# A two-stage kernel on one core: twelve intermediate tiles kept on the chip, and a new written order for its first sixty microseconds

## The chip, the cores and the metric

The kernel runs on one core of one Trainium2 chip. The metric is the device time of one execution in microseconds (us); smaller is better. The core has five engines, each with its own queue in program order: TensorE (PE; its weight loads are shown apart as PEld), VectorE (DVE), ScalarE (ACT), GpSimd (POOL) and SyncE (SP, which here issues every DMA). PE writes only to PSUM, which has eight banks of 128 x 512 floats; ACT and DVE take the results out of it.

## The reference

A retention layer (a linear attention with a decay per head) is followed by a two-layer network with SiLU. All is float32.

```python
# q, k, v: batch 4, heads 8, 768 positions, head size 64
gamma = 1.0 - 2.0 ** (-5.0 - np.arange(H))
for t in range(S):
    state = gamma * state + outer(k[:, :, t], v[:, :, t])
    y[:, :, t] = scale * q[:, :, t] @ state
x = y.transpose(0, 2, 1, 3).reshape(3072, 512)
h = x @ w_in                      # 512 x 2048
out = (h / (1 + np.exp(-h))) @ w_out   # 2048 x 512
```

## The kernel before

Retention is computed by *units*: unit n is chunk n // 4 (of six chunks of 128 positions) of batch n % 4, so there are 24. For each unit the letters of the written order stand for:

- `T(n)`: PE transposes k and q into PSUM (`kp`, `qp`), and ACT copies them out (`kt`, `qt`). `K(n)` on DVE, or `KA(n)` on ACT in eight pieces, scales k; `Q(n)` on DVE scales qt.
- `SC(n)`: PE makes sums of k and v and the scores. `A(n)`, three calls: DVE masks the scores (`am`), and the sums go into `mid` and then `state`. `SC` of the next unit uses the same banks (tag `s`), so it waits for these.
- `YA(n)`, `YB(n)`: PE's products that make y; between them stands a fence, a POOL instruction that waits for the last matmul of YA and lets YB begin.
- `X(n)`, four calls: ACT copies y out, ACT makes the first of three parts of `xt`, and DVE the second and third. (Each float32 product is done as three passes of a rounded format, so each operand is split into three parts.)
- `W(i)`: one step of turning slice i of w_in (given as 64-bit floats) into its three parts, on ACT and DVE, eleven calls in all.

The first layer has 96 *groups* (c, f): chunk c of all four batches (512 rows) times slice f of 16 of the hidden width. A group is twelve matmuls of 128 x 512 into two banks, `ha` and `hb`. `P(n)` issues such a product in the early order and `CL(n)`, three calls, closes it: ACT copies ha out with a factor (L744), DVE subtracts hb (L749), ACT applies SiLU (L754). The result, g, is 256 KB, and `put_g` stores it to DRAM (L760). Products and the transposed k share three banks in turn (`turn`). Once all groups are done, the second layer reads each g back (L773), splits it (L805 to L808) and multiplies it by w_out (L1088), chunk by chunk, 128 x 512 outputs in two banks, `oa` and `ob`. The last two slices of the last chunk are issued batch by batch at the end (L1102), so that the outputs of the first three batches are taken out meanwhile.

The order of the work: PE's order is written out by hand throughout. In the first part, up to `early_order.close()` (units 0 to 9, groups (0,0), (0,1), (0,2) and (1,0)), so is that of SP, DVE, ACT and POOL: each engine runs its instructions in the order of the source. After that a planner orders those four, held by `queue(...)` and `issue_after(...)`, which put instructions behind a named one. The later units come in *visits* between groups: a visit m does the transposes of unit m and YA of unit m - 2 in its first half, and SC of unit m - 1 and YB of m - 2 in its second. `steps` lists the remaining groups: (1,1), (1,2), (0,3), (1,3), (0,4), (1,4), then from step 6 on (0,5), (1,5), (2,0), (0,6) and so on.

On-chip room: k, q and v of units 0 to 7 share the slots of w4 to w11, the third parts of which these units fill before those slices of w_in are converted (`load`, `early`); those of later units have two or three buffers each. g has three buffers (tag `hs`).

Some narrow and full matmuls on zeros (`narrow`, `fill`) only keep PE busy at the start and in gaps.

Of the kernel before, what the change touches and what calls it, by code (L numbers as in the profile page):

```python
# [34 lines left out]
def kernel(  # L35
# [28 lines left out]
    nc = tc.nc  # L64
# [81 lines left out]
    early = {}  # L146
# [27 lines left out]
    def load_w(i):  # L174
# [8 lines left out]
        if i < NF:  # L183
            to = t.rearrange("p (i o f) -> o p i f", o=2, f=n)
            src = w_in[:, ts(i, n)].rearrange("(i o p) f -> o p i f", o=2, p=128)
            nc.sync.dma_start(out=to[0], in_=src[0])
# [139 lines left out]
    for n in range(EARLY - 2):  # L326
        for name in "kqv":
            load(name, n)
        if n in (0, 3):
            load_w(n // 3)  # L330
# [128 lines left out]
    FILL_P = {(0, 0): 1, (1, 0): 2}  # L459

# [277 lines left out]

    def close_in(*of):
        list(close_steps(*of))  # L740

    def close_steps(c, f, ha, hb):
        hs = hpool.tile([128, NT], FP32, tag="hs", name=f"g_{c}_{f}")
# [11 lines left out]
        pending.append((c, f, hs))  # L755

    def put_g(keep):
        while len(pending) > keep:
            c, f, g = pending.pop(0)
            stored[:] = [nc.sync.dma_start(out=g_dram[c, f], in_=g).ins]  # L760
# [58 lines left out]

    def T(n):  # L820
        stage_t(n)
# [36 lines left out]
    idle[:] = [banks("y", "idle")[:, 0]]  # L858
    narrow(idle[0], 39)
    fill(idle[0], 2)  # L860
    narrow(idle[0], 39)
    T(0), K(0)
    nc.scalar.activation(out=token, in_=lgc[:1, :1], func=AF.Silu)
    SC(0), A(0), Q(0), A(0), A(0)
    W(0), W(0), W(0), W(0), W(0)
    YA(0), YB(0), X(0)
    T(1), K(1)
    W(0)
    load_w(2)
    W(0)  # L870
    X(0), X(0)
    SC(1), A(1)
    W(0)
    A(1)
    Q(1), A(1)
    T(2), K(2)
    W(0), X(0)
    W(0), W(0)
    YA(1), SC(2)
    A(2)  # L880
    YB(1), X(1)
    A(2), Q(2), A(2)
    X(1)
    T(3), K(3)
    X(1), X(1)
    YA(2), YB(2), X(2)
    SC(3), A(3), A(3), Q(3), A(3)
    X(2), W(1), W(1)
    X(2), X(2)
    YA(3), YB(3), X(3), X(3)  # L890
    W(1), W(1)
    T(4)
    X(3), X(3)
    K(4)
    W(1), W(1)
    loads(EARLY - 2), loads(EARLY - 1)
# [15 lines left out]
    P(0)  # L912
    next_chunk()
    SC(4)
    CL(0), CL(0), CL(0)
    put_g(0)
    W(1)
    T(5)
    A(4), A(4), Q(4), K(5), A(4)
    W(1), W(1)  # L920
    YA(4), SC(5), YB(4)
    loads(EARLY)
    load_w(3)
    W(2), W(1)
    A(5)
    W(1), W(2), W(2)
    X(4)
    T(6)
    P(1)
    A(5), Q(5), A(5)  # L930
    KA(6)
    W(2), W(2), W(2)
    load("k", EARLY + 1), load("q", EARLY + 1)
    load_w(4)
    W(2)
    CL(1), CL(1)
    W(2)
    YA(5), SC(6), YB(5)
    X(5)
    W(2), W(2)  # L940
    A(6)
    W(2)
    CL(1)
    put_g(0)
    T(7)
    P(2)
    load("v", EARLY + 1)
    K(7), A(6), Q(6), A(6)
    X(4), X(5), X(4), X(4)
    CL(2)  # L950
    YA(6), SC(7), YB(6)
    X(6)
    T(8)
    load("k", EARLY + 2), load("q", EARLY + 2)
    A(7), A(7), Q(7)
    next_chunk()
    K(8), A(7)
    CL(2), CL(2)
    put_g(0)
    X(5), X(5)  # L960
    X(6)
    YA(7), SC(8), YB(7)
    X(7), X(7)
    A(8)
    X(6), X(6)
    T(9)
    load("v", EARLY + 2), load("k", EARLY + 3), load("q", EARLY + 3)
    X(7), X(7)
    A(8), Q(8), A(8)
    P(NF)  # L970
    KA(9)
    CL(NF), CL(NF)
    taken[0] = 3
    begin_w()
    CL(NF)
# [4 lines left out]
    next(half_visits)  # L980
# [17 lines left out]
    behind = {x: lambda: next(half_visits) for x in pairs[:-1]}  # L998
# [24 lines left out]
    for n, (c, f) in enumerate(steps):  # L1023
# [4 lines left out]
        if n in parts:  # L1028
            behind_next.append(lambda m=parts[n]: part_t(m, taken_out[0]))
        patient[0] = steps.index((3, 0)) <= n < max(turns_at) + 2  # L1030
        product_in(c, f)
        put_g(1)
        store_w()
        if (c, f) in takes:
            take_w(taken_out[0], n < len(pairs + three) or c == NC - 1)
# [119 lines left out]
```

## Time and profile before

| | |
|---|---|
| time, three runs | 613.16 us median (612.46 to 614.77) |
| the profiled execution | span 612.6 us; no other time of it is on record |
| PE, busy | 600.9 us (98%) |
| DVE, busy | 397.1 us (65%) |
| ACT, busy | 324.5 us (53%) |
| DMA | 108.90 MB, queue 62.3% of 16 engines' span |
| stores of g, reads of g | 96 and 96, 256 KB each, 3.7 and 2.7 us from issue to landing |

A timeline row reads: start, duration, engine, line, operation, out<-in, shape, count, and in brackets the idle time of the engine before it with what ended it. An entry such as SPq is the queue of an engine; the duration of a DMA there is that of its issue, and it lands some microseconds later. "Granted clock" is the share of its full clock that PE was given; it is 1.00 all through.

### The profile page before, as it was taken

The page shows a single profiled execution, that of the slowest core. Times are in us where ns is not written, and L with a number is a line of the kernel's source. Part 1 is how long each engine was busy: PE and PEld are TensorE (multiplying, and loading weights), DVE is VectorE, ACT ScalarE, POOL GpSimd, SP SyncE. Part 2 cuts the span into 40 slices and gives each one's busy share as a digit, 9 for nine tenths or more (in the row PEclk, how much of TensorE's full clock was granted, in tenths as well). Part 3 has the DMA queues.
Part 4 walks back from the last instruction along what each step waited for, and adds up shares of the span by engine and source line. Part 5 has one row for each costly group of instructions (what it writes and reads, how often), then busy time and mean ns, then how long its engine had stood idle before and what let it go on. Part 6 is the DMA issues. An engine that isn't in the chain of part 4 may idle for free.

```text
span 612.6 us, 13713 instructions
## 1 busy us (share of the span) xinstructions
PE 600.9 (98%) x5509; PEld 495.9 (81%) x5509; DVE 397.1 (65%) x672; ACT 324.5 (53%) x598; POOL 32.9 (5%) x89
## 2 busy tenths in 40 slices
PE   8898999999999999999999999999999999999997
PEld 6686788888888888888888888888888888888886
DVE  4797898678886676766689774635545463645631
ACT  7688678678676667676698632212221322313211
POOL 3000020100021111210000000000000000000000
PEclk9999999999999999999999999999999999999999
DMA  9999976586799699998777542623524433433301
GB/s 195 209 199 231 258 214 203 160 254 188 258 231 233 154 263 263 258 291 255 248 249 267 169 138 69 206 69 106 169 72 136 137 110 97 152 123 99 107 1 69
DMA packets 144336, 108.90 MB, mean 178 GB/s; under 512 B 101137, under 2 KB 109585, under 8 KB 144273
## 3 DMA queue, kind: packets, MB, share of 16 engines
q1 hardware_dynamic: 144272, 108.03, 62.3%
q8 instruction: 43, 0.70, 0.5%
q14 instruction: 21, 0.16, 0.1%
HBM read 66.06 MB, written 36.70 MB: 168 GB/s over the span
## 4 chain that ended last, share of the span: by engine, by line
PE 92%; DMA 3%; SPq 2%; DVE 2%; issue 1%; ACT 0%; DVEq 0%
PE ha L734 28%; PE o L1088 21%; PE oa L1088 14%; PE hb L734 14%; PE ob L1088 7%; PE y L562 3%; DMA qf<-in_q_dram 2%; PE sc L504 1%; SPq L166 1%; PE sc L514 1%; DMA kqv<-in_v_dram 1%; SPq L188 1%; PE o L1102 0%; PE oa L1102 0%; PE kp L485 0%
## 5 line engine op out<-in xcount | busy, mean ns | idle before, releaser
L734 PE MATMUL ha<-xt,wi 128*128 128x512 f32 x768 | 193.0, 393 | 0.0
L734 PEld LDWEIGHTS ha<-xt,wi 128*128 128x128 f32 x768 | 142.4, 188 | 30.5 <-DVE xt L636 0.2
L1088 PE MATMUL o<-wo,gs 128*128 128x512 f32 x564 | 143.1, 389 | 0.0
L805 ACT ACTIVATE gs<-gr 128x512 fp32r<-128x512 f32 x96 | 53.2, 621 | 139.0 <-issue 138.0
L1088 PEld LDWEIGHTS o<-wo,gs 128*128 128x128 f32 x564 | 105.9, 188 | 22.0
L807 DVE TENSOR_TENSOR gs<-gr,gs 128x512 fp32r<-128x512 f32 x96 | 62.1, 684 | 94.2 <-ACT gs L805 94.2
L1088 PE MATMUL oa<-wo,gs 128*128 128x512 f32 x376 | 115.7, 389 | 0.0
L749 DVE TENSOR_TENSOR g<-g,hb 128x512 f32<-128x512 f32 x96 | 65.7, 684 | 57.6 <-ACT g L744 42.6
L734 PE MATMUL hb<-xt,wi 128*128 128x512 f32 x384 | 102.7, 389 | 0.0
L734 PEld LDWEIGHTS hb<-xt,wi 128*128 128x128 f32 x384 | 72.1, 188 | 15.1
L1088 PEld LDWEIGHTS oa<-wo,gs 128*128 128x128 f32 x376 | 70.5, 188 | 14.6
L754 ACT ACTIVATE g<-g 128x512 f32<-128x512 f32 x96 | 60.3, 629 | 37.7 <-DVE g L749 37.6
L1088 PE MATMUL ob<-wo,gs 128*128 128x512 f32 x188 | 73.1, 389 | 0.0
L744 ACT ACTIVATE g<-ha 128x512 f32<-128x512 f32 x96 | 56.7, 591 | 28.6 <-PE ha L734 19.8
L808 DVE SCALAR_TENSOR_TENSOR gs<-gs 128x512 fp32r<-128x512 f32 x96 | 62.0, 683 | 0.1
L1088 PEld LDWEIGHTS ob<-wo,gs 128*128 128x128 f32 x188 | 35.3, 188 | 7.4
L205 ACT ACTIVATE ca<-wf 128x512 f32<-128x512 f32 x32 | 21.6, 675 | 6.6 <-DVE cs L218 4.0
L522 DVE TENSOR_TENSOR am<-sc,decay 128x512 f32<-128x512 f32 x24 | 16.5, 687 | 11.4 <-PE sc L514 11.4
L1112 ACT ACTIVATE o<-o 128x512 f32<-128x512 f32 x10 | 6.0, 598 | 33.4 <-PE o L1088 33.0
L218 DVE SCALAR_TENSOR_TENSOR cs<-ca,cs 128x512 uint32<-128x512 uint32 x32 | 22.7, 710 | 0.9
L639 DVE SCALAR_TENSOR_TENSOR xt<-xt 128x512 fp32r<-128x512 f32 x28 | 19.9, 715 | 0.7
L562 PE MATMUL y<-qt,mid 64*64 64x64 f32 x376 | 19.4, 220 | 0.4 <-issue 0.4
(122 smaller groups left out, 562.2 us busy)
## 6 DMA issues: line engine op xcount, KB each, us to landing
gd<-g SPq DMA_DIRECT2D x96, 256.0 KB, 3.7
gr<-gd SPq DMA_DIRECT2D x96, 256.0 KB, 2.7
wf<-in_moe_w_out_dram SPq DMA_DIRECT2D x16, 512.0 KB, 4.7
out_dram<-o SPq DMA_DIRECT2D x23, 256.0 KB, 2.1
wf<-in_moe_w_in_dram SPq DMA_DIRECT2D x16, 256.0 KB, 4.6
wf<-in_moe_w_in_dram SPq DMA_DIRECT2D x32, 128.0 KB, 4.1
kf<-in_k_dram SPq DMA_DIRECT2D x16, 256.0 KB, 4.1
qf<-in_q_dram SPq DMA_DIRECT2D x16, 256.0 KB, 4.1
```

What stands on the lines that cost most here:

```text
L205: top = nc.scalar.activation(out=a.bitcast(FP32), in_=hi.bitcast(FP32), func=AF.Abs, scale=2.0 ** -3).ins
L218: nc.vector.scalar_tensor_tensor(out=s, in0=a, scalar=3, in1=s, op0=ALU.logical_shift_left, op1=ALU.bitwise_xor)
L562: i = nc.tensor.matmul(to[ts(e, D), o, a, :], lhsT=lhsT, rhs=rhs, start=key not in started, stop=True, skip_group_check=True).ins
L639: nc.vector.scalar_tensor_tensor(out=x[2], in0=x[1].bitcast(FP32), scalar=-1.0 / EPS, in1=x[0].bitcast(FP32), op0=ALU.mult, op1=ALU.add)
L734: nc.tensor.matmul(hb if i == 2 else ha, lhsT=w_sb[f][:, i, ts(kk, 128)], rhs=xt[c][:, i, kk, :], start=kk == 0 and i != 1, stop=kk == KIN ...
L744: copied[:] = [nc.scalar.activation(out=hs, in_=ha, func=AF.Copy, scale=ONE_E).ins]
L749: taken_out[:] = [nc.vector.tensor_tensor(out=hs, in0=hs, in1=hb, op=ALU.subtract).ins]
L754: nc.scalar.activation(out=hs, in_=hs, func=AF.Silu)
L805: nc.scalar.activation(out=t[:, 0, :], in_=g, func=AF.Copy, scale=HALF)
L807: nc.vector.tensor_tensor(out=t[:, 1, :], in0=g, in1=high, op=ALU.subtract)
L808: nc.vector.scalar_tensor_tensor(out=t[:, 2, :], in0=t[:, 1, :].bitcast(FP32), scalar=-1.0 / EPS, in1=high, op0=ALU.mult, op1=ALU.add)
L1088: nc.tensor.matmul(o, lhsT=g, rhs=wo[f][:, i, :], start=f == 0 and i != 1, stop=f == NF - 1 and i != 0)
```

## The change

- Twelve g, of groups (0,0) to (0,5) and (1,0) to (1,5), go to slots of their own in SBUF, three each in those of w7, w9, w10 and w11, and are stored later, one or two at a time in steps 6 to 17 (`keep_g`, `put_later`). A late store is placed behind the last weight load or store (`last`).
- Product (1,1) comes directly behind (1,0); the first half of visit 10, which stood between them, comes behind (1,1).
- `T(n)` is split into `TK` and `TQ`, which can be placed apart, and the order of all five engines and of the loads is another from unit 4's transposes on. Ahead of that the order is the same.
- The fillers at the start are 36 and 33 narrow matmuls rather than 39 and 39 (nine matmuls with nine weight loads).
- The last batch's left half: its last four matmuls go to a bank of their own, `last_left`. ACT takes the left half of what oa holds until then, DVE subtracts ob's, then adds the new bank's; the right half is as before.

```diff
@@ load_w
-            nc.sync.dma_start(out=to[0], in_=src[0])
+            last[:] = [nc.sync.dma_start(out=to[0], in_=src[0]).ins]
@@ beside stage_t: stage_k(n) and stage_q(n) do its two halves
@@ ahead of close_in
+    keep_g = {7: [(0, 0), (0, 1), (0, 2)], 9: [(1, 0), (1, 1), (1, 2)],
+              10: [(0, 3), (1, 3), (0, 4)], 11: [(1, 4), (0, 5), (1, 5)]}
+    kept_g = [x for i in keep_g for x in keep_g[i]]
+    homes = {}
+
+    def new_g(c, f):
+        if (c, f) not in kept_g:
+            return hpool.tile([128, NT], FP32, tag="hs", name=f"g_{c}_{f}")
+        i, = (i for i in keep_g if (c, f) in keep_g[i])
+        if i not in homes:
+            homes[i] = wpool.tile([128, 3, NT], FP32, tag=f"w{i}", name=f"gk_{i}")
+        return homes[i][:, keep_g[i].index((c, f))]
@@ close_steps and put_g
-        hs = hpool.tile([128, NT], FP32, tag="hs", name=f"g_{c}_{f}")
+        hs = new_g(c, f)
...
-        pending.append((c, f, hs))
+        (later if (c, f) in kept_g else pending).append((c, f, hs))
...
+    def put_g(keep, of=None):
+        of = pending if of is None else of
+        while len(of) > keep:
+            c, f, g = of.pop(0)
+            with tc.issue_after(last[0]) if of is later else ExitStack():
+                last[:] = stored[:] = [nc.sync.dma_start(out=g_dram[c, f], in_=g).ins]
@@ the start
-    narrow(idle[0], 39)
+    narrow(idle[0], 36)
     fill(idle[0], 2)
-    narrow(idle[0], 39)
+    narrow(idle[0], 33)
@@ the order from unit 4's transposes to the end of the early part; before
-    T(4)
-    X(3), X(3)
-    K(4)
-    W(1), W(1)
-    loads(EARLY - 2), loads(EARLY - 1)
-    P(0)
-    next_chunk()
-    SC(4)
-    CL(0), CL(0), CL(0)
-    put_g(0)
-    W(1)
-    T(5)
...
-    T(7)
-    P(2)
-    load("v", EARLY + 1)
-    K(7), A(6), Q(6), A(6)
-    X(4), X(5), X(4), X(4)
-    CL(2)
-    YA(6), SC(7), YB(6)
-    X(6)
-    T(8)
-    load("k", EARLY + 2), load("q", EARLY + 2)
-    A(7), A(7), Q(7)
-    next_chunk()
-    K(8), A(7)
-    CL(2), CL(2)
-    put_g(0)
-    X(5), X(5)
-    X(6)
-    YA(7), SC(8), YB(7)
...
@@ after
+    W(1), TK(4), TQ(4), W(1), load("k",6), load("q",6), X(3), X(3), K(4), W(1), P(0)
+    load("v",6), SC(4), next_chunk(), TK(5), W(1), TQ(5), load("k",7), W(2), W(1), Q(4), A(4)
+    load("q",7), CL(0), A(4), W(1), load("v",8), load("q",8), K(5), A(4), CL(0), load("v",7)
+    W(1), W(1), load("k",8), YA(4), SC(5), W(1), W(2), A(5), W(2), CL(0), load_w(3), W(2)
+    put_g(0), YB(4), TK(6), TQ(6), P(1), X(4), A(5), KA(6), W(2), load("q",9), W(2), W(2)
+    load("k",9), W(2), CL(1), Q(5), A(5), YA(5), SC(6), YB(5), CL(1), X(5), W(2), W(2), Q(6)
+    CL(1), X(4), W(2), A(6), TQ(7), TK(7), P(2), load("v",9), X(5), K(7), A(6), load_w(4)
+    YA(6), X(4), A(6), SC(7), YB(6), A(7), X(6), Q(7), CL(2), X(4), put_g(0), X(6), TK(8)
+    A(7), CL(2), TQ(8), load("q",10), load("k",10), CL(2), YA(7), YB(7), A(7), next_chunk()
+    K(8), X(6), X(5), X(7), X(6), put_g(0), TQ(9), X(7), X(5), TK(9), KA(9), X(7), X(7), SC(8)
+    A(8), P(NF), CL(NF), A(8), A(8), load("v",10), CL(NF), load("k",11), Q(8)
@@ the visits
-    next(half_visits)
+    behind[pairs[0]] = lambda: [next(half_visits), next(half_visits)]
@@ the loop over steps
+    put_later = {6: 1, 7: 2, 9: 1, 10: 1, 11: 1, 13: 1, 14: 1, 15: 1, 16: 1, 17: 2}
...
+        if n in put_later:
+            put_g(len(later) - put_later[n], later)
@@ the tail, last batch
-                ends += [(oa, (0, 1), slice(i * DM // 2, (i + 1) * DM // 2))
-                         for i in range(2)]
+                last_left = banks("s", "o_left")[:, 0]
+                ends += [(last_left, (0, 1), slice(0, DM // 2)), (oa, (0, 1), slice(DM // 2, DM))]
...
+            left, right = (ts(i, DM // 2) for i in range(2))
+            nc.scalar.activation(out=o[:, left], in_=oa[:, left], func=AF.Copy, scale=ONE_E)
+            nc.scalar.copy(out=o[:, right], in_=ob[:, right])
+            nc.vector.tensor_tensor(out=o[:, left], in0=o[:, left], in1=ob[:, left],
+                                    op=ALU.subtract)
+            for x, cols, op in (last_left, left, ALU.add), (oa, right, ALU.subtract):
+                nc.vector.scalar_tensor_tensor(out=o[:, cols], in0=x[:, cols], scalar=ONE_E,
+                                               in1=o[:, cols], op0=ALU.mult, op1=op)
                 nc.sync.dma_start(out=out[rows, cols], in_=o[:, cols])
```

## The prediction

> **What bounds the kernel now.** I read the page first, then TensorE's (PE's) waits, then its timeline from 25 to 70 us beside the DMA queue's, and last the tail. The page:
>
> ```profile
> span 612.6 us, 13713 instructions
> PE 600.9 (98%) x5509; PEld 495.9 (81%) x5509; DVE 397.1 (65%) x672; ACT 324.5 (53%) x598; POOL 32.9 (5%) x89
> ...
> PE   8898999999999999999999999999999999999997
> ...
> DMA  9999976586799699998777542623524433433301
> ```
>
> PE is 98% busy, and falls below 9 tenths only in the first four slices (61 us), where DMA is full, and in the last. So a gain can come only from the 11.7 us in which PE is idle, and from time in which it is busy without running at its pace. The windows say more:
>
> ```profile
> 50.00:60.00 10.00, 8.10 (x167) 6.27 (x168) 9.11 (x17) 8.81 (x24) 0.00 (x0) 1.00 0.92 235
> 60.00:70.00 10.00, 10.00 (x174) 8.00 (x174) 6.62 (x12) 6.94 (x16) 2.33 (x4) 1.00 1.03 255
> ```
>
> The columns are PE, weight loads, DVE, ACT, POOL, granted clock, DMA share, GB/s. From 60 us on PE has no gap, and before it DMA, DVE and ACT are all near full at once. PE's longest waits there:
>
> ```profile
> 52.73 0.63 PE L476 MATMUL qp<-ident,qf 128*128 128x128 f32 x4 [0.26 <-DMA qf<-in_q_dram]
> 53.20 0.59 PE L317 MATMUL ha<-zero 128*128 128x512 bf16 x2
> 53.44 2.29 PE L734 MATMUL ha<-xt,wi 128*128 128x512 f32 x8
> ...
> 58.54 0.27 PE L485 MATMUL kp<-ident,qf 64*128 64x64 f32 x1 [1.09 <-DMA qf<-in_q_dram]
> ```
>
> These are unit 9's q, first-layer group (1,0), and unit 10's q. The idle marks are not the whole loss. One undisturbed period (product 36.79 to 42.60) gives the pace: a product 2.94 us (2.72 when the next is a product too), transposes .84, SC .94, YA .75, YB .35. What PE does from unit 4's transposes (25.98) to product (1,1) (59.79) sums to 27.5 by these; it took 33.8. So 6.3 us is the most that the new order can win there. The tail:
>
> ```profile
> 607.67 1.11 PE L1102 MATMUL oa<-wo,gs 128*128 128x256 f32 x8
> 607.87 0.59 ACT L1116 COPY o<-ob 128x512 f32<-128x512 f32 x1 [0.74 <-PE ob L1102]
> 608.88 0.76 DVE L1121 SCALAR_TENSOR_TENSOR o<-oa,o 128x256 f32<-128x256 f32 x2 [0.71 <-PE oa L1102]
> ```
>
> Eight half-width matmuls, four for the left half and then four for the right. Both DVE pieces start only after the eighth ends at 608.78, though the left half was complete after the fourth (about 608.3) and ACT's copy after 608.46. Somebody who reads one half of this bank waits for the writes to the other.
>
> **The change part by part.**
>
> *Fewer fillers.* Nine narrow matmuls with their nine weight loads: 39 take 1.23 us, so 9 x .0315 = .28 us ahead of unit 0's transposes. These run at 4.25, and their k was issued at .75 and took 3.4 us to land, so the fillers were all but hidden; behind them the first SC waits another .45 for v at 6.54. Worth 0. Without that cover it would be .28.
>
> *Twelve g kept.* g(0,0) and g(0,1) no longer stand in the DMA queue ahead of unit 10's loads. By issue plus time to landing, v of unit 7 lands at 42.7 and g(0,0) at 43.5: a store takes about .78 us of the queue (g(0,1) .54, after w4's last piece). Unit 9's transposes need both k and q of 9; ahead of the later of these stand the same loads in both kernels and one store less, so it lands at 52.6 - .8 = 51.8. Unit 10's k then comes after v of 9, w4 and q of 10, (1.0 + 1.75 + 1.2 + 1.1 us by the same differences) at 56.9, against 58.5 for its q before. The stores come back as twelve issues on the SP queue in steps 6 to 17, about 87 to 118 us, where the DMA share is .5 to .7. I cost them at nothing there: PE is at its pace, and the DMA engines have 6 us free in 20. What this hides behind is the slots' re-use, the third rival.
>
> *(1,1) behind (1,0).* Product (1,1) needs nothing of unit 10. It fills the 1.09 and .34 us that PE waited for unit 10's q and k, and saves one change between products and small matmuls, 2.94 - 2.72 = .22.
>
> *The new order, from unit 4's transposes on.* Engines take their queue in order, so I follow what each waits for. Up to 31.67 (unit 5's transposes) nothing differs. Then:
> - ACT: the copy of g(0,0), at 29.95 before, now stands behind both copies of unit 5 and a piece of w2, so at 33.87, and what it held back (silu, w1's and w2's pieces) comes behind it. The scaling of unit 6's k on ACT (1.92 us) moves from 37.67 to about 39.0. SC(6) on PE needs it, and the copy of g(0,1) is queued behind it, for which DVE then stands some 2 us: SC(6) starts at 41.1 instead of 40.48.
> - That and a .2 us wait for unit 6's state puts unit 8's transposes at 48.4 instead of 47.57.
> - YA(7) now waits for mid of 7, which DVE makes after two ops more (masks and Q .60 apart, mid .33): 50.65 at its end. YB(7) follows with no SC(8) between. It must wait for the POOL fence, some .55 (unit 0's YA to YB: 9.04 + .40 to 9.73 with fillers between; last matmul to POOL to PE). Unit 9's transposes start at 51.75, just as their operands land (51.8), and end at 52.65; SC(8) ends at 53.6.
> - (1,0) needs unit 7's xt. On ACT, between YB(7)'s end and that op's end, there are now next_chunk (1.18), the copy of y (.47), a copy of unit 9 (.47) and the op itself (.63): 54.45. So (1,0) starts at 54.5 instead of 53.44.
> - From there (1,0) 2.72, (1,1) 2.94, unit 10's transposes and YA(8) together 1.50 (67.01 to 68.51 in a later visit): SC(9) at 61.66, against 62.74 before. **Gain 1.1 us**, all of which reaches the end, since PE has no gap after 60 us.
>
> Bounds. From below: DMA alone (51.8, .45 for the last transposes, .95 SC(8), then the same 7.16) gives SC(9) at 60.4, a gain of 2.4. From above: three of my waits were within .1 us of not counting, and one more op (.6) or two on the way to (1,0) cost it all: -.3. I take 1.1, by the ACT rows, since they end later than the DMA's.
>
> *The last left half.* Its four matmuls go to a bank of their own, but the sums of the first 14 slices stay in oa's left half, and ACT now reads these into o with ONE_E, after which DVE subtracts and adds. The row above has a reader of the left half wait for the right half's matmuls, and ACT's new read is just such a reader. Then: PE's end 608.78, ACT 256 columns .37 (mid's copy, L528), DVE subtract .34, DVE add .41: last result at 610.05 against 609.63, **a loss of .4**. If instead ACT reads early, left is done when the right half ends, and one piece instead of two follows: 609.30, a gain of .35. In the worst order (the right half's copy of ob queued behind the waiting ACT op, DVE's right piece last) .8 is lost. I take .4, by the wait that this very bank shows.
>
> The Trainium skill, PSUM — Partial Sum Buffer, section "PSUM bank collisions raise a hardware error", says to guard PSUM by bank and quadrant, not by address, since two engines at different columns of one bank still collide. The trace agrees (.71 us of DVE idle, released by the right half's last matmul). By that rule the sum is 612.5; by addresses alone it would be 611.7.
>
> *Sum.* The profiled execution has only its span on record, 612.6 us; the three runs have 612.46, 613.16 and 614.77, so it was an ordinary one, and I carry the difference over as it is: 613.16 - 1.1 + .4 = **612.5 us**. About .5% (3.07 us) is what a measurement of this kernel can tell from no change.
>
> **The rivals.**
>
> 1. *DMA sets the pace.* ACT's and DVE's new order costs nothing and PE waits at unit 9 for its operands only: -2.4 + .4 gives 611.2, with the better tail 610.4. For it: up to 57 us the SP queue issues without a pause, and 33.8 against 27.5 us says that most loss is order. Against it: ACT has eight ops between YB(7) and (1,0) or right before. Chance .20.
> 2. *The order gives back what the stores win.* ACT and DVE, at 8.8 and 9.1 of 10 us before (1,0), lose one or two us more than in my walk: (1,0) at 55.5 to 57, time 613.5 to 615. For it: DVE then has idle time at 40 to 42 and 47 to 48 us, which it lacked before. Against it: all of the work was there before, and in 60 to 70 us DVE has 3.4 us to catch up. Chance .12.
> 3. *Slots come free late (slower).* The g live in slots of w7, w9, w10 and w11 and these weights are written into them right after the last store has been issued (the second of w7's two last stores in the very step in which w7 is taken). ACT's first write of w7 was at 98.81; 1.1 earlier is 97.7. A store that is issued at the end of step (1,5), about 92 to 93, lands 3.7 to 5.4 later: 95.7 to 98.4. If ACT stands, the copy of the next product's ha stands behind it and then PE. Three banks give 2.72 - .59 = 2.1 us of slack. Over that every us counts: a whole landing more at each of four slots is 4 x (3.7 - 2.1) = 6.4, so 619, 616.3 to 622 as it goes. For it: the four margins are one step or none. Against it: the data are long there and SP is idle in these steps. It decides from 2.1 us of wait on ACT. Chance .10.
>
> **How the numbers follow.** My forecast, 611.0 to 613.5, has .58. The third rival is slower by over .5% whenever it happens: .10. A third of the first rival (with the better tail, and scatter of the median such as the 612.46 below it) is under 610.1: .06. The rest, .84, is within. The range leaves out the third rival and the fastest corner: 610.3 to 615.2.
>
> **What would show it.** Right: PE's wait for unit 10's q gone; (1,0) starting at about 54.5, released by ACT's xt; SC(6) waiting for ACT's scaling; SC(9) at 61.7; PE without gaps from there to 603; the last DVE piece about 1.2 us after PE's end. Wrong: (1,0) starting before 53.5 (first rival) or after 55.5 (second); any wait of ACT for a store of g near 90 to 110 us followed by a gap on PE (third); ACT's new op at the tail ahead of PE's last matmul.

## The result, and the profile after

The changed kernel takes 617.86 us in the median of eight runs (615.94 to 621.01); the kernel before, on the same chip, 612.81 (611.56 to 617.07). The ratio is 1.0071, 95% interval 1.0045 to 1.0098: slower by some 4.4 us (2.8 to 6.0; the medians differ by 5.05), where I had forecast 612.5, within 610.3 to 615.2, and no change that can be told. The profiled run took 617.72 us, of which the span is 615.6, so 2.1 us lie outside it. A second profile of before (e0 below) has 1.8 us outside.

The page of the changed kernel, busy shares and slices:

```profile
span 615.6 us, 13692 instructions
PE 602.2 (98%) x5500; PEld 495.4 (80%) x5500; DVE 397.5 (65%) x673; ACT 324.6 (53%) x599; POOL 34.2 (6%) x89
...
PE   7998999999999999999999999999999999999997
...
DMA  9996867795699699999777442523523432433201
```

On this scale it is the same kernel. The difference is in places. The windows that correspond to those shown of before:

```profile
50.00:60.00 10.00, 9.70 (x167) 8.05 (x167) 8.81 (x18) 9.28 (x24) 0.09 (x1) 1.00 0.54 116
60.00:70.00 10.00, 9.22 (x229) 7.43 (x228) 8.11 (x15) 8.10 (x19) 2.31 (x4) 1.00 0.77 199
```

From 50 to 60 us PE is busier than before (9.70 us against 8.10), as the change meant it, and DMA is half empty (share .54 against .92). But from 60 to 70 us PE now has .78 us of idle time, where it had none. PE's three longest waits from 26 to 76 us (total, times, longest):

```profile
PE kp L491 <- issue: 1.5, 1, 1.5
PE kp L530 <- DMA qf<-in_q_dram: 0.8, 1, 0.8
PE y L607 <- DVE am L567: 0.5, 1, 0.5
```

The wait for unit 10's q (1.09 us) is gone. In its place stands a wait of 1.5 us for "issue", that is, for nothing that the profile shows, in the middle of unit 8's transposes, and one of .8 us for unit 11's q. The timeline of PE, its products there:

```profile
54.64 2.19 PE L779 MATMUL ha<-xt,wi 128*128 128x512 f32 x8
...
57.59 1.98 PE L779 MATMUL ha<-xt,wi 128*128 128x512 f32 x8
...
63.07 2.12 PE L779 MATMUL ha<-xt,wi 128*128 128x512 f32 x8
...
67.28 0.27 PE L530 MATMUL kp<-ident,qf 64*128 64x64 f32 x1 [0.78 <-DMA qf<-in_q_dram]
68.53 0.73 PE L779 MATMUL ha<-xt,wi 128*128 128x512 f32 x2
```

These are groups (1,0), (1,1), (1,2) and (0,3). In before they started at 53.44, 59.79, 64.06 and 68.51. So against this profile of before a gain of 1.0 us was there at (1,2), and at (0,3) nothing was left of it (.02 us later than before). Against the second profile of before (e0 below), which has (1,2) at 61.91 us, there was no gain even there. Unit 11's q was late because SP stood: the queue's own waits from 50 to 62 us have this line on top.

```profile
SPq L186 <- DVE cs L208: 5.1, 1, 5.1
```

The first piece of w5 (in `begin_w`) waits 5.1 us on SP for its buffer, and the new order has unit 11's q behind it. The next loss comes at 138 us, where ACT waits for a store. First the changed kernel's timeline of ACT, then that of before:

```profile
137.88 1.24 ACT L802 ACTIVATE g<-ha 128x512 f32<-128x512 f32 x2 [1.97 <-DMA gd<-g]
```

```profile
136.04 0.60 ACT L744 ACTIVATE g<-ha 128x512 f32<-128x512 f32 x1 [0.23 <-DMA gd<-g]
```

From the start of group 28 (of 96, counted from 0 in PE's order) to that of group 43 it takes 47.61 us, against 45.31 in before; PE is late by the sum, 2.3 us, from there to the end. Last, the tail:

```profile
610.46 0.64 PE L1094 MATMUL oa<-wo,gs 128*128 128x256 f32 x4
611.14 0.38 ACT L1117 ACTIVATE o<-oa 128x256 f32<-128x256 f32 x1 [0.58 <-PE oa L1094]
611.56 0.42 DVE L1119 TENSOR_TENSOR o<-o,ob 128x256 f32<-128x256 f32 x1 [1.07 <-DMA out_dram<-o]
611.89 0.42 DVE L1122 SCALAR_TENSOR_TENSOR o<-oa,o 128x256 f32<-128x256 f32 x1
612.23 0.41 DVE L1122 SCALAR_TENSOR_TENSOR o<-o_left,o 128x256 f32<-128x256 f32 x1
```

ACT's read of oa's left half starts after the right half's last matmul, and three pieces of DVE follow one by one.

### The profile page after: what moved, and what is told of

Same layout as the page of the kernel before. It is cut to its first block, busy times and chain, and to the rows that moved or that the text cites. A ratio compares the mean times of both kernels' runs of the same rounds, so it can differ in the third digit from the quotient of the medians.

```text
span 615.6 us, 13692 instructions
## 1 busy us (share of the span) xinstructions
PE 602.2 (98%) x5500; PEld 495.4 (80%) x5500; DVE 397.5 (65%) x673; ACT 324.6 (53%) x599; POOL 34.2 (6%) x89
## 4 chain that ended last, share of the span: by engine, by line
PE 91%; DMA 4%; DVE 1%; ACT 1%; SPq 1%; issue 1%; DVEq 0%; ACTq 0%; POOL 0%; POOLq 0%
PE ha L779 26%; PE o L1079 21%; PE oa L1079 14%; PE hb L779 13%; PE ob L1079 7%; PE y L607 4%; PE sc L549 2%; PE sc L559 2%; DMA gd<-g 1%; DMA kqv<-in_v_dram 1%; DMA qf<-in_q_dram 1%; PE kp L491 1%; SPq L166 1%; PE qp L502 0%; PE o L1094 0%
## 5 line engine op out<-in xcount | busy, mean ns | idle before, releaser
L807 DVE TENSOR_TENSOR g<-g,hb 128x512 f32<-128x512 f32 x84 | 57.5, 685 | 52.8 <-ACT g L802 40.3
L812 ACT ACTIVATE g<-g 128x512 f32<-128x512 f32 x84 | 52.8, 629 | 31.2 <-DVE g L807 31.0
L802 ACT ACTIVATE g<-ha 128x512 f32<-128x512 f32 x84 | 49.9, 594 | 25.5 <-PE ha L779 18.6
L1107 DVE TENSOR_TENSOR o<-o,o 128x512 f32<-128x512 f32 x10 | 6.8, 688 | 19.3 <-ACT o L1106 19.3
```

Of the source, the lines that this page charges most:

```text
L802: copied[:] = [nc.scalar.activation(out=hs, in_=ha, func=AF.Copy, scale=ONE_E).ins]
L807: taken_out[:] = [nc.vector.tensor_tensor(out=hs, in0=hs, in1=hb, op=ALU.subtract).ins]
L812: nc.scalar.activation(out=hs, in_=hs, func=AF.Silu)
```

## The experiments

Each time is the median of its runs, each ratio is to the kernel before as run beside it on the same chip, and each profile is of one run (the medians of before differ by up to 2.7 us from chip to chip, so only kernels that were run side by side are compared).

**e0, before once more.** No edit.

> The kernel before, unchanged, for a second profile of it. Theory: the profiled execution of before that I worked from (span 612.6 us, no time on record) was the 614.77 us one, since the changed kernel's profiled run has 617.72 us with a span of 615.6, some 2.1 us of the time lying outside the span; a median run of before then has a span of about 611 us, and the second profile shows one between 609.5 and 611.5. Rival: it was an ordinary run and before has nothing outside its span; then the span is again 612 to 613 and the time no more than .5 above it. Where PE stood in before (1.09 us for unit 10's q, and the start of group 41 at 174.7 us or so against 177.0 after) should come back within .3 us.

Measured: 612.2 us, span 610.4, so 1.8 us outside. All of the 2.15 us by which this span is shorter lie ahead of group 7 (72.78 and 70.63 us); from there on the two executions agree to .02 us. So these two differ in their first 70 us alone. Neither is ordinary: the first, with 1.8 us outside its span, would have taken some 614.4 us (an estimate; the median beside the changed kernel is 612.81), and this one took 612.2 where 29 runs of before beside it have a median of 614.15. The wait for unit 10's q did not come back as expected: .27 us here.

**e1, e2 and e3, one repair each.** e1: `load("q",11)` beside `load("k",11)`. e2: the late stores sooner. e3: ACT's read of oa early.

```diff
e1 -    CL(NF), load("q",11)
   +    ... load("k",11), load("q",11), Q(8)        (ahead of begin_w)
e2 -    put_later = {6: 1, 7: 2, 9: 1, 10: 1, 11: 1, 13: 1, 14: 1, 15: 1, 16: 1, 17: 2}
   +    put_later = {6: 1, 7: 2, 8: 1, 9: 1, 10: 1, 11: 1, 12: 1, 13: 1, 14: 1, 15: 1, 16: 1}
e3 +    (ahead of the last slices' matmuls)
   +    nc.scalar.activation(out=o_last[:, : DM // 2], in_=acc[B - 1][0][:, : DM // 2],
   +                         func=AF.Copy, scale=ONE_E)
```

> The changed kernel with one thing moved: the load of unit 11's q stands beside that of its k, ahead of the first piece of the next weight load, which waits for a buffer. Theory (the load of q behind the waiting weight load costs the gain of the early part, 1.0 us): q of 11 is issued before 56 us and lands by 63.5, PE's wait of .8 us for it at 66 to 68 us is gone, group (0,3) starts at 67.5 instead of 68.53, and the time is 1.0 us below the changed kernel's, if the queue of 120 to 140 us stays as it is. Rival A: the .4 and 1.9 us of 138 to 176 us are waits for transfers that follow their own clock; PE, 1 us early, then waits 1 us longer there, and the time is the same (0 +- .3). Rival B: DMA is full up to 67 us, so that q lands no sooner or v of 11 or a weight piece is late instead: PE waits as long near 66 us, 0.

> The changed kernel with its twelve late stores given out one step sooner: at 6, 7 (two), and then one in each of 8 to 16, rather than 6, 7 (two), 9, 10, 11, 13, 14, 15, 16, 17 (two), so that the last lands at 116 us instead of 125. Theory (the last of them run into the dense loads of 118 to 135 us, a g store then lands 2 us late, ACT stands 1.97 us for it, PE loses .4 at 138 and 1.9 by 176): ACT's wait at 136 to 138 us falls below .5 us, group 29 starts within .1 of group 28's spacing in before, group 41 starts 1.5 to 2.3 us sooner than the changed kernel's (177.0), and the time is 1.5 to 2.3 us below its. Rival: the queue is full from 122 to 134 us anyhow, or the planner's order of ACT and DVE makes the loss: the wait stays over 1 us, the time is within .5 us of the changed kernel's.

> The changed kernel with ACT's read of the left half of oa moved in the source ahead of the last slices' matmuls (its output tile is made there too), so that it doesn't wait for the right half's matmuls in the same bank. Theory (a reader of a half bank waits for all writes to this bank that stand ahead of it in the source): ACT reads oa while PE is still at the last slices, 6 us or more before its end, PE isn't held up, and the last DVE piece ends .5 to .9 us after PE's last matmul rather than 1.54; the time is .6 to 1.0 us below the changed kernel's. Rival: the matmuls to the right half of oa now wait for ACT's read (the same bank, in the other direction), or the last DVE chain of three sets the end rather than ACT: PE stands .5 us or more ahead of the last eight matmuls, or the DVE end stays 1.2 us or more behind PE's; within .3 us of the changed kernel.

Measured: ratios to before 1.006 (1.0034 to 1.0087), 1.0065 (1.0038 to 1.0093) and 1.0055 (1.0034 to 1.0076). None takes more than a part of the loss away. In its profile each did in its place what it should: in e1 the wait for unit 11's q is gone, in e2 ACT's wait at 138 us is gone, in e3 the span ends 3.70 us after PE's last matmul rather than 4.46 (3.78 in before). But the "issue" wait is in all three, 2.1, 1.5 and 1.8 us long, at one and the same place. And in e2 groups 28 to 43 still took 46.52 us. The larger part was something that none of the three touched.

**e4 to e7, one part of the change each, on the kernel before.** e4 keeps the twelve g; e5 is the changed kernel with no g kept and the old tail, which leaves the order, the fillers and (1,1) behind (1,0); e6 has the new tail alone; e7 has (1,1) behind (1,0) alone.

```diff
e5 -    keep_g = {7: [(0, 0), (0, 1), (0, 2)], ...}
   +    keep_g = {}
e7 -    next(half_visits)
   +    behind[pairs[0]] = lambda: [next(half_visits), next(half_visits)]
```

> The kernel before, with the twelve g kept and stored late, and nothing else of the change. Theory (the stores move from a stretch where PE waits for loads to one where ACT then waits for stores): the early part ends .8 to 1.4 us sooner, since two stores (.78 and .54 us) no longer stand ahead of unit 10's loads; from the start of group 28 to that of group 43 (45.31 us in both profiles of before, 47.61 in that of the changed kernel) it takes 46.5 to 47.6 us; the time is .3 to 1.5 us above before. Rival: the loss at 136 to 180 us is made by the new order or by the place of (1,1); then the 45.31 us stay, and the time is .8 to 1.4 us below before.

> The changed kernel with no g kept (each stored as soon as it is closed, as before) and with the tail of before: what is left is the new order, (1,1) behind (1,0), and the fillers. Theory (the late stores make the loss from 136 us on; the order itself wins nothing): from group 28 to group 43 it takes 45.31 us, as before; group 7 starts 45.3 to 47 us after group 0, against 44.1 and 45.3 in the two profiles of before; the time is 0 to 2 us above before. Rival A (my prediction's walk: the order is worth a gain): group 7 starts under 44.5 us after group 0, time 0 to 1 us below before. Rival B (the order of ACT and DVE makes the loss later): 46.5 us or more from group 28 to 43.

> The kernel before with the changed tail alone: the last left half in its own bank, ACT reading oa's left half behind all matmuls. Theory (ACT's read waits for the right half's matmuls in the same bank, and a chain of three follows; .69 us in the span and .35 us between the span's end and the time, 2.12 against 1.77): from PE's last matmul to the last DVE piece 1.54 us rather than .85, span to time 2.1 rather than 1.77, and the time 1.0 us above before. Rival: the .35 us is chance of other runs: the time .7 us above; or the tail costs nothing in the time, because the store ahead sets the end: 0.

> The kernel before with product (1,1) directly behind (1,0) and the first half of visit 10 behind it, and nothing else of the change. Theory: the product fills the 1.09 and .34 us in which PE waited for unit 10's q and k and saves .22 us of change, so group (0,3) starts 1.4 to 1.7 us sooner relative to group 0 (41.0 in the profile of before), and this stays to the end: the time is 1.4 to 1.7 us below before. Rival: PE then comes to unit 11's transposes before their q has landed (62.74 us), as in the changed kernel (.8 us of wait there), or ACT and DVE, full in 50 to 70 us, hold up (0,3): .5 us below before or no change.

Measured: 1.0015 (.9988 to 1.0042), 1.0064 (1.0036 to 1.0091), .9992 (.9973 to 1.0010), .9999 (.9979 to 1.0019).

- e4 did what its theory said in the trace: group 7 at 43.64 us after group 0 (44.09 and 45.26 in before), groups 28 to 43 in 46.57 us. The loss holds; the gain isn't shown, since e14 below, with the same first part, has 44.87, and e6 and e7 have 44.57 and 45.85.
- e6: from PE's last matmul to the span's end 4.47 us, .70 more than in e0. The time doesn't show them (1.7 us less to .6 more).
- e7: PE has no wait for unit 10's q or k. The time did not move.
- e5, the order, the fillers and the pair without the rest, has nearly the whole loss.

e7's trace (of a run that took 615.64 us; the median is 613.74) shows what to look for. It has the order of before up to there, and yet PE stands 1.8 us at unit 7's y. First e7, then e0, PE's timeline:

```profile
51.98 0.37 PE L562 MATMUL y<-qt,state 64*64 64x64 f32 x1 [1.80 <-issue]
...
52.61 1.11 PE L476 MATMUL kp<-ident,kf 128*128 128x128 f32 x4
53.51 1.06 PE L476 MATMUL qp<-ident,qf 128*128 128x128 f32 x4
```

```profile
50.49 0.66 PE L476 MATMUL kp<-ident,kf 128*128 128x128 f32 x4
50.98 0.60 PE L476 MATMUL qp<-ident,qf 128*128 128x128 f32 x4
```

Two costs: the stand itself, and then unit 9's transposes at half pace, since the granted clock falls to .50 from 52 to 54 us. I counted the instructions of PE's queue up to each "issue" wait, over the whole span, in every trace: matmuls, weight loads, and its 61 to 65 semaphore instructions and drains, without which the counts don't come out. Where an expectation below says "matmul or weight load", this count is meant. Waits of .3 us and more:

| kernel | "issue" wait, us, at PE's n-th instruction |
|---|---|
| before | .39 at 962, .43 at 1218 |
| e0, e6, e7 | none; .37 at 962; 1.80 at 2498 |
| e4 | .65 at 962, .41 at 2498 |
| after, e3 | 1.52 and 1.81 at 2242 (each with .34 at 962) |
| e1, e2 | 2.08 and 1.50 at 2242 (e1 also 1.01 at 450, .39 at 706) |
| e5 | 1.18 at 962, 1.27 at 2242, .33 at 2498 |

All these numbers are 194 plus a multiple of 256 (to within one, where two start together), and so are those of the kernels further below: 48 waits of .3 us and more in twenty traces (52 with the shorter ones), and no "issue" wait of a matmul stands elsewhere. The two of before, which its first profile had:

```profile
22.20 0.33 PE L562 MATMUL y<-qt,mid 64*64 64x64 f32 x5 [0.39 <-issue]
...
27.06 0.60 PE L476 MATMUL qp<-ident,kqv 128*128 128x128 f32 x4 [0.43 <-issue]
```

The queue named q8 in the page carries 43 packets of 16 KB, as many as PE's 11,000 instructions have 256es:

```profile
q8 instruction: 43, 0.70, 0.5%
```

So PE's code comes in pieces of 256 instructions, and PE stands where a piece ends before the next has come. In the changed kernel PE passed its 1986th instruction at 45.63 us; the next piece travelled from 46.85 to 48.11, with the DMA share at 1.24 from 46 to 48 us; PE had run through the 256 instructions in 2.7 us and stood from 48.32 to 49.84. (1.2 us to the start of the transfer, 1.3 on the way and 1.7 from landing to PE make 4.2; the 2.7 us of work hide that much of it.) The Trainium skill, Runtime: NRT & Kernel Launch, section "Instruction fetch mechanics", has the block of 16 KiB and 256 instructions, which these traces bear out, and calls the cost of its boundary mostly hidden, which they do not: here it is up to 2.1 us.

**e8 to e11, the fillers.** The change has 18 PE instructions fewer at the start, so from there on each piece holds other work. The traces show it in the first piece. With 39 and 39 fillers (before, e0, e4, e6, e7, e9, e14) PE passes its 194th instruction at 5.6 to 5.9 us, ahead of unit 0's scores, and the next piece travels from 6.2 to 6.7 us on. With 36 and 33 (after, e1, e2, e3, e5, e8) the 194th comes with these scores, at 6.4 to 6.6 us, and the piece travels from 9.0 to 9.9 on. The scores, which wait for their v, begin at 6.3 to 6.7 us either way, but the 450th instruction comes at 9.8 to 10.0 us in the first case and at 12.4 to 13.2 in the second. e8: the fewer fillers alone on before. e9: the old fillers in the changed kernel. e10 and e11: 24 and 32 narrow matmuls more in the changed kernel, ahead of unit 1's transposes of q.

```diff
e8     (before)         -    narrow(idle[0], 39) ... narrow(idle[0], 39)
                        +    narrow(idle[0], 36) ... narrow(idle[0], 33)
e9     (after)          the reverse
e10    (after, stage_q) +    narrow(u, 24 if n == 1 else 0)       (e11: 32)
```

> The kernel before with 36 and 33 narrow fillers for 39 and 39 at the start, nothing else. In the traces PE takes its instructions in pieces of 256 (16 KB each), and stands on 'issue' only where one of these begins: in all five profiles with the new order for 1.3 to 2.1 us at the 2242nd matmul or weight load, in those of the old order for .2 to .4 (four of five none or under .45, one 1.8 at the 2498th). Theory (the 18 instructions fewer shift what stands in each piece; where a piece of short matmuls is run through in 2.2 to 3 us, the next, some 4.2 us after the last boundary, comes too late): with the old order the piece that ends at the 2242nd becomes one of 2.2 us rather than 3.0; PE stands 1 to 2 us on 'issue' at the 2242nd or the 2498th, unit 4's transposes start .5 to 1 us later than in before's profiles (25.2 us in the mean; 26.1 with the new order), and the time is 1 to 2.5 us above before. Rival (the place of the boundaries is of no account, the stalls go with the loads of the new order): 'issue' stays under .5 us, the time within .5 us of before.

> The changed kernel with before's 39 and 39 fillers, nothing else undone. Theory (the same): the piece that ends at the 2242nd matmul or weight load takes 3.3 us and more rather than 2.7, and PE's stand on 'issue' there falls from 1.3 to 2.1 us to .3 to 1.0; unit 4's transposes start at 25.0 to 25.5 rather than 26.1 in the mean; the time is 1 to 2 us below the changed kernel's, some 2 to 3 above before. Rival (the fillers cost and save nothing, as I predicted): 1.3 us and more of 'issue' as before, the time as the changed kernel's.

> The changed kernel with 24 narrow matmuls on zeros more (48 instructions with their weight loads, .76 us) ahead of unit 1's transposes of q, where PE waits 1.3 us for that q. Theory: the boundaries move 48 instructions back in the work. By the changed kernel's own trace its pieces then take 6.1, 2.2, 6.1 and 4.7 us: the 2242nd is no place to stand any more (under .3 us of 'issue' there), and the short piece is the one that ends at the 1986th, where PE stands 1 to 2.5 us on 'issue'. Time about as the changed kernel's. Rival: the stall goes with unit 8's transposes whatever the count: 1.3 us or more on 'issue' right at them.

> The same with 32 rather than 24 (64 instructions, 1.0 us): 16 instructions further, and by the changed kernel's trace no piece from 17 to 62 us is run through in under 3.9 us. Theory: no 'issue' wait over .5 us between 30 and 75 us at all, group (1,0) starts 1.3 to 2 us sooner after group (0,0) than in the changed kernel (27.7 to 29.4 us), and the time is 1 to 2 us below the changed kernel's. Rival: PE stands 1.3 us or more on 'issue' at some place anyhow (the code comes late because DMA is full, at whichever boundary), or the next wait takes over (unit 11's q, .8 to 1.2 us): the time as the changed kernel's.

Measured: 1.006 (1.0036 to 1.0083), 1.0078 (1.0048 to 1.0109), 1.015 (1.0118 to 1.0182), 1.015 (1.0122 to 1.0179). e8 gives one answer: nine fillers fewer, which I had put at 0, cost 3.3 us by themselves (617.12 against 613.81). Its three longest waits from 20 to 76 us, and its windows with the clock in the third column from the end (the profiled run took 620.08 us, 6.3 above before's median, so its losses are larger than the 3.3):

```profile
PE y L562 <- issue: 2.1, 1, 2.1
PE kp L476 <- issue: 1.8, 1, 1.8
PE sc L504 <- issue: 1.2, 1, 1.2
```

```profile
56.00:58.00 2.00, 1.53 (x15) 1.41 (x16) 0.76 (x2) 1.11 (x2) 0.00 (x0) 0.83 0.65 176
58.00:60.00 2.00, 2.00 (x6) 1.44 (x5) 1.82 (x4) 2.00 (x8) 0.00 (x0) 0.50 1.10 246
```

They are at 2498, 2242 and 962, and after the longest the clock is at half. The other three were misses as repairs. In e9 the fillers' part came back (the first piece travels from 6.34 us on, and group 0 starts at 26.41 us, 27.2 in the mean of after, e1, e2 and e3), but PE stood 1.86 us at 2242 all the same, now at the last matmuls of YB(6), and the clock then lay at .50 to .61 from 50 to 56 us. The changed kernel with the old fillers is still 5.0 us above before, so the rest of the change loses as much without the fillers' part, and the two don't add up. Since e4, e6 and e7 cost 1.2 us or less each, I put it down to the order; no run has the new order alone. In e10 and e11 the waits moved: e10 has 1.43 at 450, 1.58 at 1218 and still 1.21 at 2242, e11 .71 at 450, .65 at 1730, .46 at 1986 and .99 at 2242. So I could say where PE can stand, always at such a boundary, and not at which it will: the piece's transfer began .2 us after the last boundary in e14 and 4.7 in e15, and a count of the work in a piece doesn't tell that. I take it to go by what the DMA queues hold just then; no run shows it.

**e12 to e15.** e12 and e13 take instructions away on before and keep PE busy as long; e14 is e4 with the sooner stores; e15 has the repairs of e1, e2 and e3 and 103 narrow fillers at the start.

```diff
e12 -    narrow 39, fill 2, narrow 39
    +    narrow 36, fill 2, fill(idle[0][:, :256], 1), narrow 33
e13 +    narrow 9, fill 6, narrow 9
e15 (after, with e1, e2, e3)
    -    narrow 36, fill 2, narrow 33
    +    narrow 103
```

> The kernel before with nine narrow fillers (36 and 33 for 39 and 39) replaced by one filler of 256 columns, so that PE is busy as long at the start (9 x 26.6 ns = .24 us against some .2 us) but executes 16 instructions fewer. Theory (it is the place of the 256-instruction boundaries): as with the fillers left out, PE stands on 'issue' for 1 to 2 us at the 962nd, 2242nd or 2498th matmul or weight load, and the time is 1.5 to 3.3 us above before. Rival (the .24 us less of fillers makes PE wait longer for the first loads, its clock falls to half and the rest follows): the time is that of before within .7 us, 'issue' under .5 us in sum after 20 us.

> The kernel before with sixty narrow fillers replaced by four full ones (9, six full, 9 for 39, two full, 39): as long (60 x 26.6 ns = 1.6 us against 4 x .40), 112 instructions fewer. Theory: by the second profile of before, the pieces of 256 would then take 4.1, 5.5, 5.5, 3.0, 8.4 and 4.8 us from 27 us on, one short piece (to the 2242nd) in place of two (3.0 and 3.7); the share of runs that stand there is no higher than before's, and the time is between 1 us below before and .5 above. Rival (any shift costs, since the fillers' number was matched to the order, or the clock needs narrow ones): 1.5 us or more above before.

> The kernel before with the twelve g kept, and the late stores given out one step sooner than in the change (6, 7 twice, 8 to 16 one each). Theory: the early gain (group 7 at 43.6 us after group 0, against 44.1 to 45.3 in before) stays, ACT's wait for a store near 136 us does not come, and groups 28 to 43 take 45.3 us rather than 46.57; with .35 us more outside the span the time is .3 to 1.5 us below before. Rival: a transfer that takes 1.4 us longer near 165 us (seen with the sooner stores in the changed kernel) costs 1.2 us at group 41 again, or PE stands on 'issue' as often: .3 below to 1.2 above before.

> The changed kernel with unit 11's q loaded ahead of the waiting weight load, the stores one step sooner, ACT's read of oa ahead of the last matmuls, and 103 narrow fillers in place of 36, two full, 33 (as long, 64 instructions more, so that by its own trace no piece of 256 from 17 to 62 us takes under 3.98 us). Theory (the losses are these: 1.3 to 2.1 us of 'issue', .8 at unit 11, 1.2 to 2.3 from 136 to 180 us, .69 at the end): the time comes down by 2.5 to 4 us from the changed kernel's, to within 1 us of before. Rival (the code's transfer waits up to 3.4 us behind full DMA queues, so that PE stands at some boundary wherever it lies; the slow transfer at 165 us stays): at most 1.5 us down, 2 us or more above before.

Measured: 1.0071 (1.0045 to 1.0097), 1.0069 (1.0046 to 1.0091), .9997 (.9978 to 1.0017), 1.0108 (1.0078 to 1.0138). e12 separates the two causes left: with the fillers' time kept (they end at 4.08 us; 4.12 in before, 3.87 in e8) and 16 instructions fewer the loss is there in full, 4.3 us, with waits of 1.1 at 2242 and 2.0 at 2498:

```profile
PE y L562 <- issue: 2.5, 2, 2.0
PE kp L476 <- issue: 1.1, 1, 1.1
```

Its 194th instruction comes at 6.53 us and the piece travels from 9.77 on, as with the fillers left out. So it is the count, not the .24 us. e13 was a miss: its time, 2.7 us above before, is the rival's (any shift costs). Its profile, of a run of 615.40 us, has nothing over .31 us early, but a wait at instruction 5314, again 194 plus a multiple of 256, in a visit where no other kernel stands. What its other runs lose isn't shown (in nine of the twelve the mean clock was below .998; this profile has .999):

```profile
184.48 0.65 PE L514 MATMUL sc<-qt,kt 64*64 64x64 f32 x32
186.86 0.27 PE L562 MATMUL y<-qt,state 64*64 64x64 f32 x1 [1.73 <-issue]
```

e14's groups 28 to 43 take 45.31 us, so the sooner stores do mend the old order; its profile had the 1.85 us at 2498 all the same, and the time is that of before. e15 has no wait for q, 45.3 us for groups 28 to 43 and 3.69 us at the end, all three repairs as meant, and loses more at other places: 1.53 us at 2242, .48 at 1986, a clock of .63 from 10 to 20 us, and 2.2 us between groups 43 and 77. No version is faster than before by more than the noise.

**e16 and e17, the loss at 160 to 180 us.** e2, e5, e8 and e12 lose 1.0 to 1.2 us from group 28 to 43, although no store is in the way. In those four traces the piece of PE's code travels 29.0 to 29.8 us after group 28's start, and the two reads of yr (y of one chunk, put into DRAM and read back), issued at 26.5 to 27.3, land after 5.5 to 5.7 us; in five that lose nothing there (before, e0, e6, e7, e14) it travels at 24.2 to 24.7, and they land after 4.1 to 4.6. Two more kernels put the nine matmuls back, ahead of unit 13's transposes: e16 is e8 with them, e17 is e2 with them.

```diff
+                narrow(tp[i], 9 if (n, i) == (3 * B + 1, 0) else 0)
```

> The kernel before with 36 and 33 fillers, and the nine narrow matmuls left out there put ahead of unit 13's transposes, at about 80 us. Theory (a transfer of PE's code among other transfers makes them land late): from there on the boundaries lie as in before, the code travels some 24.5 us after group 28's start, the reads of yr land after 4.1 to 4.6 us and groups 28 to 43 take 45.31 us (46.51 with the fillers left out alone), while the early waits on 'issue' (1 us or more in sum at the 962nd, 2242nd or 2498th) stay: the time is .5 to 1.2 us below that kernel's 3.3 above before. Rival (the place of the code is chance, the late start makes it): 46.2 us or more again.

> The changed kernel with the late stores one step sooner and nine narrow matmuls ahead of unit 13's transposes. Theory: groups 28 to 43 take 45.3 to 45.5 us, rather than 46.52 with the sooner stores alone and 47.6 in the changed kernel, so that of its loss only the early part (2242nd instruction, unit 11's q) and the tail are left: the time is 1 to 2 us below the changed kernel's. Rival: 46.2 us or more again, the time as with the sooner stores alone (4.0 us above before).

Measured: e16 1.0021 (1.0005 to 1.0036), e17 1.0067 (1.0043 to 1.0091). In e16 the code travels 24.5 us after group 28's start and groups 28 to 43 take 45.31 us, as forecast. The reads of yr in the DMA issues (KB each, median us to landing), first of e8, then of e16:

```profile
yr<-yd SPq DMA_DIRECT2D x2, 256.0 KB, 5.7
```

```profile
yr<-yd SPq DMA_DIRECT2D x2, 256.0 KB, 4.2
```

The early waits stay (1.2 at 962, 1.8 at 2242), and the time, 1.2 us above before, is the part that they keep. So e16 bears out that a transfer of code that falls among loads delays them too. In e17 the code travelled at 24.3, but groups 28 to 43 took 46.25 us and yr landed after 5.0 and 5.2: a miss, and what delays the loads there is open. (There the piece was on its way for 2.0 us, from 24.3 to 26.3; in e16 for 1.0.)

## Why the prediction was wrong

- **"Fewer fillers: worth 0."** This step failed: 3.3 us by itself (e8). I costed nine matmuls by their .28 us and asked what hides it, and that part was right: unit 0's scores begin no later. That they are also 18 places in a stream that is fetched by 256 was in the trace of before: two waits for "issue" of about .4 us, and a queue of instruction packets. I passed over both. The same gap is in the next step: no term of the sum has PE waiting for its code, and with the old fillers put back (e9) the new order stands at the same place.
- **"The new order: gain 1.1 us, all of which reaches the end."** (1,0) started at 54.64 (forecast 54.5), and (1,2) .99 us sooner than in the first profile of before, but 1.16 later than in the second. That the forecast of (1,0) came out is luck. SC(6) began at 40.09, not 41.1, and unit 8's transposes at 47.89 (forecast 48.4); then PE stood 1.52 us, which the walk did not have, and unit 9's transposes began at 52.27 (51.75). "All of which reaches the end" failed at once: .8 us for unit 11's q (1.2 in e2), as I did not ask what stands on SP's queue behind `begin_w`.
- **"Twelve g kept ... I cost them at nothing there."** The early half is open: e4 is early, e14 isn't. The late half failed: not by the slots of my third rival, for which ACT didn't wait, but by the last stores, after which ACT waits up to 1.97 us for a store (why it lands late, among the loads of 118 to 135 us, is argued, not shown). Given out sooner, they save 1.26 us in the old order (e4 and e14) and 1.1 in the new (after and e2). With the late ones the stretch from group 28 to 43 is 1.1 to 2.9 us longer than in before (seven kernels); of the 2.3 in after, the 1.2 that e2 keeps are not the stores'.
- **"(1,1) behind (1,0)."** The wait for unit 10 went (e7), but in e0 that wait was .27 us, not 1.43: I had priced it from an execution that was late there, and the time of e7 shows no gain.
- **The tail.** The mechanism was right (ACT's read waits for the other half's matmuls), the size off: .70 us rather than .4. I had counted one DVE piece after the subtraction; it was two, with the right half's ahead of the left's, as in my "worst order" of .8. (The terms as I wrote them add up to 609.90, not 610.05.) Started early, ACT's read costs nothing (e3: 3.70 us), but gains only .08.
- **The span and the time.** I took the span of the profiled execution for its time and so for an ordinary one. In every run with its time on record 1.7 to 2.2 us lie outside the span, so it was a late one (e0).

The pieces in spans: group 7 starts 2.35 us later in the mean of after, e2 and e3 than in that of before, e0, e6 and e7 (73.96 and 71.6); 1.7 to 2.3 us from there to group 43 (after, e3); .7 at the tail; .35 outside the span. That is 5.1 to 5.7, against 4.4 (2.8 to 6.0) measured. The first of these is rough: the single profiles lie from 72.80 to 75.12 and from 70.63 to 72.78. The .35 us outside I cannot place: the other kernels with kept g have it (2.11 to 2.15 us in the median of each, against 1.75 to 1.80), and e3 hasn't.

## What to carry to other kernels

An instruction that costs no time still has a place in PE's code. Where PE runs many short matmuls while DMA is full, look for waits on "issue", count the instructions up to each, and treat any edit that adds or drops PE instructions ahead of them as a change to everything behind. Which count is a good one I could not say beforehand: of those that were tried none was better than before's. When a kernel's executions differ, take a second profile before pricing a wait of half a microsecond; and of each load that is moved, ask what stands ahead of it on its queue waiting for a buffer.

## What the runs showed of the hardware

- PE takes its code in pieces of 16 KB, 256 instructions. In the 48 waits of .3 us and more the piece had started .8 (e12) to 4.7 us (e15) after PE passed the boundary before, was on its way .9 to 1.7 us, and PE went on 1.2 to 1.8 us after it had landed.
- Stands of 1.80 (e7), 1.81 (e3), 1.86 (e9) and 2.07 us (e8) were followed by a granted clock of .50, for 3.4 us or, in e9, 6.8; those of 1.52 (after), 1.85 (e14), 2.02 (e12) and 2.08 (e1) weren't. So their length alone doesn't decide. The Trainium skill, TensorE: Matmul & The Clock Gate, Part 1, gives an idle window of about 3.4 us, free-running, before the clock halves; here under 2.1 us of idle was enough in some runs. The mean clock was below .998 in 10 of e8's 12 runs and in 7 of the 17 of before beside it.
- Where such a piece travelled among other loads, these landed some 1.4 us later (e2, e5, e8, e12), and moving the boundary away undid it in e16, though not in e17.
